# Attention's transposes split by head into pairs, and the early weight pieces spread over more units

## The chip, the cores and the metric

The kernel runs on one core of one Trainium2 chip. Its time is the device time of one execution in microseconds (us): before the change 389.75 us, the median of three runs (389.58 to 389.85). The core has a matrix engine (TensorE, PE in the profile; its weight loads are shown apart as PEld), VectorE (DVE), ScalarE (ACT), GpSimd (POOL), and SyncE (SP), which here issues nearly all DMA transfers. TensorE writes to PSUM, which has eight banks of 512 fp32 columns; the other data stands in SBUF, both with 128 partitions.

## The reference

Three layers follow each other, all in fp32.

```
y[t]  = r[t] @ (state + (u*k[t]) v[t]^T)          # 4 batches, 8 heads, 768 steps, head size 48
state = w * state + k[t] v[t]^T
x = y as 3072 tokens x 384
logits = x @ phi                                   # 32 slots, 8 experts of 4
d = softmax over tokens, c = softmax over slots
slot_out[e] = relu((d.T @ x)[e] @ w1[e]) @ w2[e]   # w1: 384 x 1024, w2: 1024 x 384
x = c @ slot_out
out = (relu(x @ w_in) ** 2) @ w_out                # 384 -> 2048 -> 384
```

## The kernel before

**Stages.** Up to about 28 us the kernel starts up; until about 127 us it computes the attention and, woven in, the softmax over the tokens; until about 160 us the experts; then the last layer, whose products take TensorE to the end.

**Attention in units.** A unit is one batch and a pair of heads: 16 units, four per batch. A unit's 768 steps are cut into NC = 6 chunks of 128. The recurrence is written as products: inside a chunk, A = K R^T (with decays multiplied in) is masked and multiplied with V; between chunks a state of 48 x 48 per head is carried by a scan. The data of a unit comes in one load of 1344 KB (`load_unit`, line 87): r and v with the steps on the partitions, and r and k turned, with head 0 in rows 0 to 47 and head 1 in rows 64 to 111.

**Even and odd chunks.** The chunks of a unit go through two PSUM banks, YE (even chunks) and YO (odd chunks), called `YB[0]` and `YB[1]`. `inter` (line 316) and `intra` (line 325) write the attention's result there, turned: head size on the partitions, steps on the columns. ScalarE copies each bank to `xT` (line 328). In the odd bank the two heads have changed places. The name kvp stands for one more bank, in which `KV` (line 298) builds the states in columns 0 to 287, and ps_tr for one that is free for short uses.

**Transposes.** `turns(x, k)`, lines 235 to 257, does two jobs with one set of banks. For the unit x (the one just finished) it turns `xT` back, so that the steps stand on the partitions, in `xn`, which the softmax stage reads. For the unit k (two ahead) it turns the decayed k into `kn`, which `pr2` on GpSimd and `KV` read one unit later. A full call has six transposes for each job, each of one chunk with both heads at once: 112 rows, of which 96 are used. They go to YE, YO and ps_tr; five copies of ScalarE (lines 252, 255, 257) take them out.

**The order of the work.** The order on each engine is written out by hand in one loop over the units n. TensorE does in this order: A(n, odd); `turns(n-1, n+2)`; in units 5, 9 and 13 four transposes more, `both` (line 373); A(n+1, even); `L(n-1)`, the logits (line 337); in units 6, 10 and 14 `soft3`; `inter(n)`; `KV(n+1)`; `intra(n)`, even and odd. A writes the two banks of ps_A (line 286), head 0 to the one and head 1 to the other; there is one ps_A. `cp` on VectorE (line 290, a COPY_PREDICATED) takes A out of it. VectorE does: `weigh(n+1)`, `cp(n, odd)`, `decay(n+3)`, `cp(n+1, even)`, `decay(n+2)`, `scan(n+1)`. In units 4, 8 and 12 ScalarE has the exponent of the softmax and one copy more (lines 348 and 350) between its copies of YE and YO. In the text below A(n, 1) stands for the odd chunks of unit n and A(n, 0) for the even ones.

**Loads.** At the end of unit n, SP issues the load of unit n+5 (five slots), and after it some pieces of 512 KB of the first eight expert weights (line 197): 24 pieces, of which three go at the start and 21 after units 0 to 10. From unit 11 on there are no more units to load; then come the other expert weights, 1536 KB each (line 194), into the slots that the units leave, and the first part of w_in.

The lines that set the places of these are, in the loop:

```
if n > 0 or nx2:
    turns(n - 1 if n > 0 else None, n + 2 if nx2 else None)
...
if nxt:
    A(n + 1, 0)
    cp(n + 1, 0)
```

Of the kernel before, what the change touches and what calls it, by code (L numbers as in the profile page):

```python
# [17 lines left out]
def rwkv_softmoe_ffn(ctx: ExitStack, tc: tile.TileContext, un, k0, wt, u, phi, w1, w2, w_in, w_out, out):  # L18
    nc = tc.nc
    NU, NPC, _, PW = un.shape  # L20
    H, D = u.shape
    NP = H // 2
    B = NU // NP
    DM, NTOK = out.shape
    S = NTOK // B
    NC = S // 128
    HC = NC // 2
# [7 lines left out]
    NB = 5  # L35
# [13 lines left out]
    def ps(tag, banks=1):  # L49
        cnt[0] += 1  # L50
        return psum.tile([128, 512 * banks], F32, name=f"ps_{tag}{cnt[0]}", tag=tag, bufs=BANKS.get(tag, 1))
# [8 lines left out]
    def take(i, dt=F32):  # L60
        if i in early:
            return early.pop(i)
        cnt[0] += 1
        slots[i] = const.tile([128, 3072], dt, name=f"slot{i}_{cnt[0]}", tag=f"slot{i}", bufs=1)
        return slots[i]
# [9 lines left out]
    def t_view(n):  # L75
        return units[n % NB][:112, ON:ON + OT].rearrange("p (m c t) -> p m c t", m=2, c=NC)
# [17 lines left out]
    def part_of(sh, rows, at, shape):  # L94
        n = 1
        for x in shape:
            n *= x
        dims = "abcd"[:len(shape)]
        return sh[:rows, at:at + n].rearrange(f"p ({' '.join(dims)}) -> p {' '.join(dims)}", **dict(zip(dims, shape)))
# [5 lines left out]
    xn = [part_of(sh0, 128, 0, [NC, DM + 1]), att.tile([128, NC, DM + 1], F32, name="xn1")]  # L105
# [14 lines left out]
    ident = const.tile([128, 128], F32, name="ident")  # L120
# [15 lines left out]
    st = {}  # L136
# [48 lines left out]
    def load_weight(i, cs=None):  # L185
        kind, e = W[i]
        if W[i] not in wt_of:
            t = take(home[i])
            wt_of[W[i]] = t.rearrange("p (c f) -> p c f", c=3) if kind == "w1" else t.rearrange("p (c d) -> p c d", c=8)
            st["raw", i] = t.rearrange("p (c f) -> p c f", c=3)  # L190
        t = st["raw", i]
        src = w1[e].rearrange("(c p) f -> c p f", p=128) if kind == "w1" else w2[e]
        if cs is None:
            nc.sync.dma_start(t, src.rearrange("c p f -> p c f"))
        else:
            for c in cs:
                nc.sync.dma_start(t[:, c], src[c])

    kvp = ps("kv")
    YB = [ps("YE"), ps("YO")]  # L200
# [10 lines left out]
    for i in range(6):  # L211
        n = 1 << i
# [19 lines left out]
    def heads(p):  # L232
        return p.rearrange("p c (h x) -> p c h x", h=2)[:, :, :, :D]

    def turns(x, k):
        banks = [YB[0], YB[1], ps("tr")]
        banks = [p.rearrange("p (c e) -> p c e", c=4) for p in banks]
        tail = [[NC - 2], [NC - 1], list(range(NC - 2))]
        if k is not None:
            kn = st[k, "kn"] = kns[(k + 1) % 2]  # L240
        for par, p in enumerate(banks):
            if x is not None and par < 2:
                for i in range(HC):
                    nc.tensor.transpose(p[:, i, :112], st[x, "xT"][:, par, i], ident[:112, :112])  # L244
            if k is not None:
                for j, c in enumerate(tail[par]):
                    nc.tensor.transpose(p[:, HC * (par < 2) + j, :112], t_view(k)[:, 1, c], ident[:112, :112])
        for par, p in enumerate(banks):
            if x is not None and par < 2:
                b, hp = divmod(x, NP)  # L250
                dst = xn[b % 2][:, par::2, 2 * D * hp:2 * D * (hp + 1)].rearrange("p c (h d) -> p c h d", h=2)
                nc.scalar.copy(dst[:, :, ::-1] if par else dst, heads(p[:, :HC]))
            if k is not None:
                if par < 2:
                    nc.scalar.copy(kn[:, NC - 2 + par], heads(p[:, HC:])[:, 0])
                else:
                    nc.scalar.copy(kn[:, :NC - 2], heads(p))  # L257

    def pr1(n):
        rv = r_view(n)  # L260
        nc.gpsimd.tensor_tensor(rv, rv, UT[:, n % NP].unsqueeze(1).to_broadcast([128, NC, 2, D]), ALU.mult)  # L261
# [5 lines left out]
    def weigh(n):  # L267
        dg = wk([128, 2, NC], "dg", 2)
        nc.vector.reduce_sum(dg, r_view(n).rearrange("p c h d -> p h c d"), axis=AX.X)
        st[n, "dg"] = dg  # L270

    def diag(n, par):
        at = wk([128, 2, HC, 128], "AT", 3, pool=att)
        st[n, "AT", par] = at
        dg = st[n, "dg"][:, :, par::2]
        nc.gpsimd.affine_select(out=at, in_=dg.unsqueeze(3).to_broadcast([128, 2, HC, 128]),  # L276
                                pattern=[[0, 2], [0, HC], [1, 128]], compare_op=ALU.is_equal, fill=0.0,
                                base=0, channel_multiplier=-1)

    def A(n, par):  # L280
        tv = t_view(n)
        p = ps("A", 2).rearrange("p (h x) -> p h x", h=2)[:, :, :HC * 128].rearrange("p h (c t) -> p h c t", c=HC)
        for i in range(HC):
            for h in range(2):
                rows = slice(64 * h, 64 * h + D)
                nc.tensor.matmul(p[:, h, i], tv[rows, 1, 2 * i + par], tv[rows, 0, 2 * i + par], start=True, stop=True)  # L286
        st[n, "A", par] = p

    def cp(n, par):
        nc.vector.copy_predicated(st[n, "AT", par], mask.unsqueeze(1).unsqueeze(1).to_broadcast([128, 2, HC, 128]),  # L290
                                  st.pop((n, "A", par)))
# [95 lines left out]
    def c_exp(b):  # L387
        nc.scalar.activation(cnat[:, b], cnat[:, b], AF.Exp)
# [87 lines left out]
    loads = [[] for n in range(NU)]  # L476
    pieces = [(i, c) for i in range(NEARLY) for c in range(3)]
    for _ in range(3):
        i, c = pieces.pop(0)
        load_weight(i, (c,))  # L480
    NL = NU - NB
    for j, pc in enumerate(pieces):
        loads[j * NL // len(pieces)].append(pc)
    for n in range(NU):
        nxt = n + 1 < NU
        nx2 = n + 2 < NU
        nx3 = n + 3 < NU
        prev = n // NP - 1
        hp = n % NP
        if n == 2:  # L490
            sel = const.tile([128, 4, NS], F32, name="sel")
            nc.vector.reduce_sum(sel, ident.rearrange("p (q s) -> p s q", q=4).unsqueeze(1).to_broadcast([128, 4, NS, 4]), axis=AX.X)
            rm = const.tile([128, E], F32, name="rm")
            nc.vector.reduce_sum(rm, ident.rearrange("p (q e j) -> p e q j", q=4, e=E), axis=AX.XY)
            ones = const.tile([1, 4], F32, name="ones")
            nc.gpsimd.memset(ones, 1.0)
        A(n, 1)
        if prev >= 0 and hp == 2:
            c_exp(prev)
        if nx2:  # L500
            pr1(n + 2)
        if nxt:
            weigh(n + 1)
            diag(n + 1, 0)
        cp(n, 1)
        if prev >= 0 and hp == 2:
            c_sum(prev)
        if n > 0 or nx2:
            turns(n - 1 if n > 0 else None, n + 2 if nx2 else None)
        if prev >= 0 and hp == 1:  # L510
            both(prev)
            soft1d(prev)
        if nx2:
            pr2(n + 2)
        if nx3:
            decay(n + 3, 1)
# [3 lines that stand above are left out]
        if n > 0:  # L520
            L(n - 1)
        if prev >= 0 and hp == 2:
            soft3(prev)
        if prev >= 0 and hp == 0:
            soft1a(prev)
            soft1c(prev)
        if prev >= 0 and hp == 1:
            c_max(prev)
        if nxt:
            diag(n + 1, 1)  # L530
        inter(n)
        if nxt:
            KV(n + 1)
        if nx2:
            decay(n + 2, 0)
        if nxt:
            scan(n + 1)
        intra(n, 0)
        if prev >= 0 and hp == 0:
            soft1b(prev)  # L540
        intra(n, 1)
        if prev >= 0 and hp == 1:
            c_sub(prev)
        if prev >= 0 and hp == 2:
            c_div(prev)
            soft4(prev)
        if n + NB < NU:
            load_unit(n + NB)
            for i, c in loads[n]:
                load_weight(i, (c,))  # L550
        else:
            if n == NU - 2:
                load_win(0, take(NSLOT, I32))
            if n == NU - 1:
                load_weight(NSLOT)
            load_weight(NEARLY + n - NL)
# [7 lines left out]
    p = ps("kv")  # L564
# [6 lines left out]
    p = ps("kv")  # L571
# [9 lines left out]
    for c, bank in enumerate((YB[0], YB[1], ps("A", 2))):  # L581
        p = bank[:96, :cols[c].stop - cols[c].start]
# [167 lines left out]
    p = ps("tr")  # L750
# [102 lines left out]
    for i, (sg, f, half) in enumerate(order):  # L853
# [42 lines left out]
        for j, k in mms:  # L896
            o = acc[half][j]
            nc.tensor.matmul(o, (hi, lo, hi)[k][:, 128 * j:128 * (j + 1)], (gh, gh, gl)[k],  # L898
                             start=(f == 0 and k == 0), stop=(f == NF - 1 and k == 2))
            if f == NF - 1 and k == 2:  # L900
                tok = 512 * (2 * sg + half)
                os = oss[(3 * (2 * sg + half) + j) % 5]
                if i < NI - 2:
                    for e in range(2):
                        c = slice(256 * e, 256 * e + 256)
# [60 lines left out]
```

## Time and profile before

| | |
|---|---|
| median of the runs | 389.75 us (389.58 to 389.85) |
| profiled execution | 390.21 us, span of its instructions 388.5 us |
| busy share of the span | PE 97%, PEld 78%, DVE 69%, ACT 52%, POOL 28% |
| mean granted TensorE clock | 0.978 of full speed |
| DMA | 66.25 MB, 171 GB/s over the span |

The profile page divides the span of one execution; a timeline gives each run of like instructions with its start, its length and, in brackets, the idle time of its engine before it and what ended that. A group such as `ps_A<-slot` names the tile written and the tile read, with the buffer numbers left out. Products on PE are pipelined: the next one starts before the one ahead has ended, so a row's length is from the first start to the last end, and one product's own length is longer than the distance to the next.

### The profile page before, as it was taken

The numbers are of one execution on the slowest core, as the hardware profiler recorded it, in microseconds if no ns is written. First come the engines' busy times: TensorE is split into PE (matmuls) and PEld (weight loads), VectorE is DVE, ScalarE is ACT, GpSimd is POOL, SyncE is SP. The second block draws the span as 40 slices with busy tenths as digits, with TensorE's granted clock in tenths as the row PEclk, the third lists the DMA queues.
The fourth block names the chain that finished last, engine by engine and source line by source line (L and its number), as shares of the span: only waits on it lengthen the run. The fifth ranks groups of instructions, "written<-read, shape, count | busy, mean of one in ns | idle before, by whom it ended". The sixth has DMA issues, their size and how long they took to land.

```text
span 388.5 us, 8227 instructions
## 1 busy us (share of the span) xinstructions
PE 376.7 (97%) x3339; PEld 303.2 (78%) x3339; DVE 268.0 (69%) x437; ACT 203.0 (52%) x422; POOL 108.6 (28%) x115
## 2 busy tenths in 40 slices
PE   6889999999999999999999999999999999999996
PEld 4778888887887655688787888888888888888884
DVE  5669788788874368589987677665665676566663
ACT  2213343444252333399787866555555565555553
POOL 4566675867761312043422240000000000000000
PEclk9559999999999999999999999999999999999999
DMA  6979999999969999813242203000000040000004
GB/s 237 390 295 356 387 375 379 329 391 311 334 200 364 412 372 397 299 55 98 84 104 90 64 0 139 24 0 0 2 1 0 2 163 0 2 0 0 2 1 163
DMA packets 23174, 66.25 MB, mean 171 GB/s; under 512 B 3296, under 2 KB 4832, under 8 KB 23136
## 3 DMA queue, kind: packets, MB, share of 16 engines
q1 hardware_dynamic: 22848, 65.38, 45.7%
q8 instruction: 26, 0.43, 0.4%
q10 hardware_dynamic: 288, 0.34, 0.3%
q14 instruction: 12, 0.10, 0.1%
HBM read 60.21 MB, written 4.72 MB: 167 GB/s over the span
## 4 chain that ended last, share of the span: by engine, by line
PE 92%; DMA 4%; DVE 2%; issue 1%; ACT 0%; ACTq 0%; DVEq 0%
PE ps_A L898 25%; PE ps_Y L898 9%; PE ps_kv L898 8%; PE ps_lg L898 8%; PE ps_A L286 7%; PE ps_tr L803 6%; PE ps_YO L316 3%; PE ps_YE L325 3%; PE ps_YO L325 3%; PE ps_A L618 3%; PE ps_Y L639 3%; DMA slot<-in_un_dram 3%; PE ps_kv L298 2%; PE ps_lg L337 2%; PE ps_YE L244 2%; DMA slot<-in_u_dram 2%
## 5 line engine op out<-in xcount | busy, mean ns | idle before, releaser
L827 DVE TENSOR_TENSOR slot<-slot,slot 128x512 fp32r<-128x512 f32 (+1 forms) x97 | 69.5, 717 | 53.3 <-PE ps_A L898 18.6
L898 PE MATMUL ps_A<-slot,slot 128*128 128x512 f32 x432 | 105.8, 389 | 0.0
L898 PEld LDWEIGHTS ps_A<-slot,slot 128*128 128x128 f32 x432 | 81.0, 188 | 17.2 <-ACT slot L824 0.3
L824 ACT CAST slot<-slot 128x512 fp32r<-128x512 f32 (+1 forms) x97 | 59.7, 616 | 49.5 <-DVE slot L821 49.2
L814 ACT ACTIVATE slot<-ps_tr 128x512 f32<-128x512 f32 (+1 forms) x97 | 57.5, 593 | 22.9 <-PE ps_tr L803 22.0
L821 DVE TENSOR_TENSOR slot<-slot 128x512 f32<-128x512 f32 (+1 forms) x71 | 48.4, 683 | 11.5 <-ACT slot L814 11.3
L898 PE MATMUL ps_Y<-slot,slot 128*128 128x512 f32 x144 | 55.4, 391 | 0.0
L898 PE MATMUL ps_kv<-slot,slot 128*128 128x512 f32 x144 | 55.1, 389 | 0.0
L898 PE MATMUL ps_lg<-slot,slot 128*128 128x512 f32 x144 | 55.0, 389 | 0.0
L290 DVE COPY_PREDICATED AT<-mask,ps_A 128x768 f32<-128x768 int32 x32 | 33.8, 1055 | 16.9 <-PE ps_A L286 9.8
L803 PE MATMUL ps_tr<-slot,slot 128*128 128x512 f32 x96 | 37.4, 391 | 0.4 <-DVE slot L767 0.4
L276 POOL TENSOR_SCALAR_AFFINE_SELECT AT<-dg 128x768 f32<-128x768 f32 x32 | 28.3, 887 | 31.8 <-PE ps_YE L325 30.3
L286 PE MATMUL ps_A<-slot 48*128 48x128 f32 x384 | 32.2, 303 | 4.7 <-DVE slot L230 3.1
L683 POOL TENSOR_TENSOR slot<-wf,slot 128x384 fp32r<-128x384 f32 x16 | 22.3, 1395 | 51.6 <-ACT slot L678 49.6
L286 PEld LDWEIGHTS ps_A<-slot 48*128 48x128 f32 x384 | 25.7, 200 | 10.9 <-DVE slot L230 3.7
L230 DVE TENSOR_TENSOR slot<-slot,ps_tab 112x768 f32<-112x768 f32 (+1 forms) x34 | 30.2, 894 | 5.1 <-DMA slot<-in_un_dram 5.1
L898 PEld LDWEIGHTS ps_Y<-slot,slot 128*128 128x128 f32 x144 | 27.0, 188 | 5.9 <-issue 0.4
L898 PEld LDWEIGHTS ps_kv<-slot,slot 128*128 128x128 f32 x144 | 27.0, 188 | 5.7
L898 PEld LDWEIGHTS ps_lg<-slot,slot 128*128 128x128 f32 x144 | 27.0, 188 | 5.5
L328 ACT COPY xT<-ps_YE 112x384 f32<-112x384 f32 x16 | 7.7, 479 | 43.3 <-PE ps_YE L325 43.3
L265 POOL TENSOR_TENSOR slot<-slot,slot 128x576 f32<-128x576 f32 x16 | 22.7, 1416 | 7.7 <-ACT slot L257 7.6
L261 POOL TENSOR_TENSOR slot<-slot,slot 128x576 f32<-128x576 f32 x15 | 21.3, 1421 | 0.3 <-ACT slot L458 0.3
(192 smaller groups left out, 503.6 us busy)
## 6 DMA issues: line engine op xcount, KB each, us to landing
slot<-in_un_dram SPq DMA_DIRECT2D x15, 1344.0 KB, 7.8
slot<-in_w_dram SPq DMA_DIRECT2D x24, 512.0 KB, 8.8
slot<-in_w_dram SPq DMA_DIRECT2D x8, 1536.0 KB, 9.4
slot<-in_w_in_dram SPq DMA_DIRECT2D x4, 1536.0 KB, 8.4
wo<-in_w_out_dram SPq DMA_DIRECT2D x16, 384.0 KB, 3.2
out_dram<-slot SPq DMA_DIRECT2D x18, 256.0 KB, 2.1
slot<-in_un_dram SPq DMA_DIRECT2D x3, 448.0 KB, 6.7
slot<-slot SPq DMA_DIRECT2D x48, 16.0 KB, 1.9
```

The lines of the kernel that those rows point to most:

```text
L230: nc.vector.tensor_tensor(x, x, t.unsqueeze(1).to_broadcast(list(x.shape)), ALU.mult)
L265: nc.gpsimd.tensor_tensor(rv, rv, st[n, "kn"] if by is None else by, ALU.mult)
L276: nc.gpsimd.affine_select(out=at, in_=dg.unsqueeze(3).to_broadcast([128, 2, HC, 128]), pattern=[[0, 2], [0, HC], [1, 128]], compare_op=ALU ...
L286: nc.tensor.matmul(p[:, h, i], tv[rows, 1, 2 * i + par], tv[rows, 0, 2 * i + par], start=True, stop=True)
L290: nc.vector.copy_predicated(st[n, "AT", par], mask.unsqueeze(1).unsqueeze(1).to_broadcast([128, 2, HC, 128]), st.pop((n, "A", par)))
L325: nc.tensor.matmul(p[o:o + D, i], vv[:, 2 * i + par, h], at[:, h, i], start=False, stop=True, skip_group_check=True)
L803: nc.tensor.matmul(p, gst[:, 128 * f:128 * (f + 1)], cTall[:, 512 * g:512 * (g + 1)], start=True, stop=True)
L814: nc.scalar.activation(fs[i, "hr"][:, c], fs[i, "p"][:, c], AF.Relu)
L821: nc.vector.tensor_mul(gg, hr, hr)
L824: nc.scalar.copy(part(i, "gh")[:, c], fs[i, "gg"][:, c])
L827: nc.vector.tensor_tensor(part(i, "gl")[:, c], fs[i, "gg"][:, c], fs[i, "gh"].bitcast(F32)[:, c], ALU.subtract)
L898: nc.tensor.matmul(o, (hi, lo, hi)[k][:, 128 * j:128 * (j + 1)], (gh, gh, gl)[k], start=(f == 0 and k == 0), stop=(f == NF - 1 and k == 2))
```

## The change

`turns` no longer turns both heads of a chunk at once. Each transpose has the 48 rows of one head (rows 0 to 47, or 64 to 111) and 48 moving columns. The transposes of the two heads are issued in pairs, and the two of a pair write different banks: for x, head rows 0 to 47 go to YE and head rows 64 to 111 to YO; for k, the one half goes to ps_tr, of the other two chunks to YO and four to columns 288 to 479 of the kvp bank. The chunks of x are taken even, odd, even, odd. Five copies of ScalarE remain, with other cuts; `turned` gives the place in `xn` for each half, over even and odd chunks. The second part of the change lets the 21 weight pieces run over units 0 to 13; in units 11 to 13 they are issued ahead of the 1536 KB loads.

```diff
+    def turned(x, a):
+        b, hp = divmod(x, NP)
+        v = xn[b % 2][:, ::2, D * (2 * hp + a):D * (2 * hp + a + 1)].unsqueeze(2)
+        pairs = [list(e) for e in v.ap]
+        return bass.AP(v.tensor, v.offset, [pairs[0], pairs[1], [DM + 1 - 2 * D * a + D, 2], pairs[3]])
+
     def turns(x, k):
-        banks = [YB[0], YB[1], ps("tr")]
-        banks = [p.rearrange("p (c e) -> p c e", c=4) for p in banks]
-        tail = [[NC - 2], [NC - 1], list(range(NC - 2))]
+        rows = [slice(64 * a, 64 * a + D) for a in range(2)]
+        todo = [[], []]
+        if x is not None:
+            px = [YB[a][:, :NC * D].rearrange("p (i q d) -> p i q d", q=2, d=D) for a in range(2)]
+            for a in range(2):
+                todo[a] += [(px[a][:, i, q], st[x, "xT"][rows[a], q, i]) for i in range(HC) for q in range(2)]
         if k is not None:
             kn = st[k, "kn"] = kns[(k + 1) % 2]
-        for par, p in enumerate(banks):
...
+            to = [ps("tr")[:, :NC * D], YB[1][:, NC * D:NC * D + 2 * D], kvp[:, NC * D:NC * D + 4 * D]]
+            to = [p.rearrange("p (c d) -> p c d", d=D) for p in to]
+            parts_k = [(0, slice(0, NC), to[0]), (1, slice(0, 2), to[1]), (1, slice(2, NC), to[2])]
+            for a, cs, p in parts_k:
+                todo[a] += [(p[:, i], t_view(k)[rows[a], 1, c]) for i, c in enumerate(range(NC)[cs])]
+        for pair in zip(*todo):
+            for a, (o, i) in enumerate(pair):
+                nc.tensor.transpose(o, i, ident[rows[a], rows[a]])
+        for a in range(2):
+            if x is not None:
+                nc.scalar.copy(turned(x, a), px[a])
+        if k is not None:
+            for a, cs, p in parts_k[1:] + parts_k[:1]:
+                nc.scalar.copy(kn[:, cs, a], p)
...
-        loads[j * NL // len(pieces)].append(pc)
+        loads[j * (NL + 3) // len(pieces)].append(pc)
...
         if n + NB < NU:
             load_unit(n + NB)
-            for i, c in loads[n]:
-                load_weight(i, (c,))
-        else:
+        for i, c in loads[n]:
+            load_weight(i, (c,))
+        if n + NB >= NU:
```

## Rows read from the trace of the kernel before

**Rows 1.** The page's chain that ended last, by engine

```profile
PE 92%; DMA 4%; DVE 2%; issue 1%; ACT 0%; ACTq 0%; DVEq 0%
```

**Rows 2.** Timeline of unit 12: start us, length us, engine, line, tiles, form, count

```profile
100.93 0.94 PE L286 MATMUL ps_A<-slot 48*128 48x128 f32 x12
...
101.80 0.51 PE L244 MATMUL ps_YE<-ident,xT 112*128 112x112 f32 x3
101.97 1.07 DVE L290 COPY_PREDICATED AT<-mask,ps_A 128x768 f32<-128x768 int32 x1 [0.66 <-POOL AT L276]
...
102.62 0.55 PE L247 MATMUL ps_tr<-ident,slot 112*128 112x112 f32 x4
...
103.10 0.94 PE L286 MATMUL ps_A<-slot 48*128 48x128 f32 x12
```

**Rows 3.** Timeline of unit 3, the copy and the next A

```profile
41.72 1.06 DVE L290 COPY_PREDICATED AT<-mask,ps_A 128x768 f32<-128x768 int32 x1 [0.84 <-POOL AT L276]
...
42.85 0.38 PE L286 MATMUL ps_A<-slot 48*128 48x128 f32 x2
```

**Rows 4.** Timeline of unit 14, which has six transposes

```profile
113.92 0.94 PE L286 MATMUL ps_A<-slot 48*128 48x128 f32 x12
...
114.98 1.05 DVE L290 COPY_PREDICATED AT<-mask,ps_A 128x768 f32<-128x768 int32 x1 [0.70 <-PE ps_A L286]
...
115.14 0.45 PE L244 MATMUL ps_YO<-ident,xT 112*128 112x112 f32 x3
...
116.08 0.49 PE L286 MATMUL ps_A<-slot 48*128 48x128 f32 x3 [0.49 <-DVE AT L290]
```

**Rows 5.** Timeline of unit 13, with `both` (L373) between transposes and A

```profile
107.72 0.49 ACT L328 COPY xT<-ps_YO 112x384 f32<-112x384 f32 x1
...
108.32 1.06 DVE L290 COPY_PREDICATED AT<-mask,ps_A 128x768 f32<-128x768 int32 x1 [0.44 <-PE ps_A L286]
...
109.34 0.49 PE L373 MATMUL ps_lg<-ident,el 96*128 96x96 f32 x4
...
109.76 0.38 PE L286 MATMUL ps_A<-slot 48*128 48x128 f32 x2
```

**Rows 6.** Single products, ns min/median/max; and timeline of KV and end sum

```profile
L244 PE MATMUL ps_YE<-ident,xT x48: 259/259/318, 28.7 to 127.2; 112*128 112x112 f32 x48
L286 PE MATMUL ps_A<-slot x384: 272/272/579, 10.7 to 122.2; 48*128 48x128 f32 x192
105.36 0.66 PE L298 MATMUL ps_kv<-slot,slot 128*48 128x48 f32 x20
L591 PE MATMUL ps_kv<-m,P x12: 276/276/297, 130.4 to 131.7; 96*128 96x32 f32 x12
130.43 1.52 PE L591 MATMUL ps_kv<-m,P 96*128 96x32 f32 x12
```

**Rows 7.** Chain of waits at the end of the start: start us, us, what

```profile
20.23 0.95 DVE AT L290
...
21.23 1.65 PE ps_A L286 x12
```

**Rows 8.** DMA by stretch (last columns share, GB/s); late weights; VectorE's waits; chain

```profile
34.00:60.00 26.00, 25.85 (x456) 22.03 (x452) 22.27 (x29) 10.29 (x32) 18.13 (x18) 1.00 1.00 379
104.00:120.00 16.00, 15.51 (x283) 12.46 (x283) 10.90 (x17) 6.28 (x19) 8.09 (x8) 1.00 0.78 275
L194 SPq DMA_DIRECT2D slot<-in_w_dram x8: 367/368/379, 101.0 to 136.8; - x8
DMA to landing us min/median/max: 6.2/9.4/14.8
152.30 5.30 PE ps_Y L639 x64
DVE slot L658 <- PE ps_kv L655: 2.7, 1, 2.7
DVE wf L157 <- DMA wo<-in_w_out_dram: 0.8, 1, 0.8
```

More of the change, by code (lines that the diff above doesn't have):

```diff
@@ L239, in turns @@
+    def turns(x, k):
+        rows = [slice(64 * a, 64 * a + D) for a in range(2)]
[4 more added lines that the diff above has]
+                todo[a] += [(px[a][:, i, q], st[x, "xT"][rows[a], q, i]) for i in range(HC) for q in range(2)]
         if k is not None:
             kn = st[k, "kn"] = kns[(k + 1) % 2]
-        for par, p in enumerate(banks):
[L242 to L255, printed above, removed]
-                else:
-                    nc.scalar.copy(kn[:, :NC - 2], heads(p))
+            to = [ps("tr")[:, :NC * D], YB[1][:, NC * D:NC * D + 2 * D], kvp[:, NC * D:NC * D + 4 * D]]
@@ L548, in rwkv_softmoe_ffn @@
             load_unit(n + NB)
-            for i, c in loads[n]:
-                load_weight(i, (c,))
-        else:
+        for i, c in loads[n]:
+            load_weight(i, (c,))
+        if n + NB >= NU:
             if n == NU - 2:
```

## The prediction

> **What bounds the kernel now.** I read the page's chain first: PE is 92% of the chain that ended last [rows 1]. Taken alone that says that any TensorE time saved is time won. So I went on to the stretch that the change touches, the 16 attention units, and read the timeline of one whole unit, 12, instead of the shares [rows 2]. Its PE order is A(12,1), twelve transposes (`turns`), A(13,0), L, and on. A(12,1) starts at 100.93 and A(13,0) at 103.10: 2.17 us. The reader is to see two things in that gap. PE fills it: the twelve transposes run from 101.80 to 103.17. And VectorE fills it too: the masked copy `cp` (L290) reads ps_A from 101.97 to 103.04, and A(13,0) overwrites ps_A, of which there is only one buffer. A(13,0) starts 0.06 after that copy ends. The same stands in units 1 to 4, 6 to 8 and 10 to 12, ten units, where the distance is 0.05 to 0.07 each time; unit 3 is shown [rows 3].
>
> Which of the two holds A back? Unit 14 answers: it has six transposes instead of twelve (there is no unit 16 to prepare), its last one starts at 115.14 + 0.45 - 0.26 = 115.33 (0.26 is a transpose's own length), and yet A(15,0) waits 0.49 us on PE for the copy and starts 0.05 after it ended [rows 4]. From the start of A to the start of the next A it takes 116.08 - 113.92 = 2.16 us, although half of the transposes are gone. That is the floor: A, copy, A. So in ten units PE's transposes and the copy end together, and cutting only the transposes buys nearly nothing.
>
> Three units differ, 5, 9 and 13. There four more transposes (L373, `both`) stand between `turns` and A, and A starts at 109.76 where the copy ended at 109.38 [rows 5]. There PE alone is late, by 0.38 - 0.05 = 0.33 us; units 5 and 9 read the same to 0.02.
>
> **The change part by part.** *Transposes.* A full `turns` has 12 transposes of 112 rows and 112 moving columns; the change makes 24 of 48 rows and 48 moving columns, in 12 pairs. Before, one follows the other at (0.55 - 0.26)/3 = 0.096 us [rows 2, 6], 1.06 us from the first to the last start, plus 0.06 for the first load (the longest takes 318 ns, the usual one 259) [rows 6].
> After, no row has a pair of transposes. The nearest: A runs two 48-row products beside each other, in two banks, 12 in 0.94 us; with 0.27 for the last and 0.10 for the first load (its first pair takes 0.38, the usual 0.27) that is 0.114 us for a pair with 128 moving columns [rows 2, 3, 6]. KV, with 48 moving columns and loads of 48, takes 0.66 us for ten pairs with the whole length of the last [rows 6], some 0.05 a pair without it: the low end. The end sum, with 32 moving columns and single loads of 128 columns, takes (1.52 - 0.276)/11 = 0.113 us each [rows 6]: the high end, if the two loads of a pair go together. I take 0.063, since a pair is bound by its load of 128 columns, a transpose's load shows as 0.06, and A shows two row halves loading together. So 12 pairs need 0.06 + 11 x 0.063 = 0.75 us where 1.11 were needed.
> In the ten units PE is done some 0.45 us before the copy and waits. What is late next is the copy, which needs A's last product (0.1 us after A's end) and 1.06 us of VectorE. Gain: what A now starts above 0.054 after the copy, 0 to 0.02 in each, 0.08 us for all ten.
> In units 5, 9 and 13 the new order has a wait of its own: the first pair already writes bank YO, so it cannot start before ScalarE has copied YO, and in these units that copy ends late, at 107.72 + 0.49 = 108.21 [rows 5]; the old order begins with YE, copied earlier. Behind that pair on PE stand all others, `both` and A. With 0.05 from ScalarE to PE, as from VectorE to PE in rows 4, the first pair starts at 108.26, the last at 108.26 + 0.06 + 11 x 0.063 = 109.01. Before, the last of the twelve started 0.10 ahead of `both`, at 109.24, so from the last transpose to A it took 0.52. Now `both` (96 rows) follows 48-row work, and a change of that kind costs: from the last transpose's start to A's it is 0.19, against 0.096 inside the run [rows 2]. I add 0.1: A at 109.01 + 0.62 = 109.63, 0.13 earlier than 109.76. Bounds: 0 and 0.33 (the copy). Three units: 0.4 us, 0 to 1.0.
>
> The Trainium skill, TensorEngine Tiling (Array Packing), section Key Properties, says that a change of tiling mode drains the engine. It speaks for the change between A and `turns`, which would then share a mode, and against it at `both`, a new change; without that drain the three units would give 0.7 instead of 0.4. The 0.19 against 0.096 agrees with it.
>
> *ScalarE.* Five copies of 1152 elements a partition in all, as before (288, 96, 288, 96 and 384 against 288, 288, 96, 192 and 288). Their ends move by a tenth at most; behind the last one waits only POOL's product, whose own result is first read in the unit after. Zero.
> *Start and end.* The start is bound elsewhere: A(1,0) at 21.23 follows the copy on VectorE [rows 7], which stands behind VectorE's work on the unit loads. In unit 15 the next work that needs `turns` is inter, behind ScalarE's copies of xn, and both copies then wait for all six pairs instead of three transposes of one bank; six pairs need about what three old ones took. Zero, or six times what a pair is slower than 0.063, which is +0.3 at 0.113.
> *Weight pieces.* 21 pieces of 512 KB after units 0 to 13, not 0 to 10: by unit 10 17 are issued instead of 21. On SP the last four now stand ahead of the 1.5 MB weight loads that follow units 11 to 13; those wait for a unit to free its slot (the first goes at 101.0 [rows 8]), and SP has nothing else in that time, so four more issues delay none of them. What they can delay is on the DMA queues. DMA was 100% busy from 34 to 60 us and 78% from 104 to 120 [rows 8], so the pieces go where there is room. The list of waits from 28 to 124 us has none on a unit load, so relief buys nothing. If the later loads slip: the last w2, issued at 136.8 and landed at most 14.8 later, at 151.6, is used in the last quarter of the downs that start at 152.30 and take 5.30, so some 4.6 us remain; the first w_out, for which VectorE waits 0.8, has 2.7 us of VectorE's idle time behind it [rows 8]. Four pieces are 2.1 MB, at 379 GB/s 5.5 us, of which the idle 22% of 16 us take 3.5; a slip of 2 us is left, under both margins. Zero, at worst +0.5, should it come on top of another delay.
>
> Sum: -0.08 - 0.4 = -0.5 us on the profiled 390.21 us (span 388.5 and 1.7 around it); the median of the runs, 389.75, is 0.46 below that execution, and I take the difference to it: **389.3 us**.
>
> **The rivals.**
> *Faster: the three units give all they can.* No drain at `both`, pairs near 0.05: 3 x 0.33 + 0.08 = 1.1 us, 388.65. For it: KV's 0.05. Against it: the late YO copy, and loads of 128 columns.
> *Much faster: the copy doesn't hold A.* Then 0.45 to 0.55 us in each of 14 units, 7 us, 382.5. Against it: unit 14.
> *Slower: the pairs are slow.* A starts late from the point where the last pair starts after 102.99 (103.10 less 0.11): with a first start at 101.71 (0.114 after A's last, 101.60) from (102.99 - 101.77)/11 = 0.111 us a pair. If a transpose's load costs what the end sum's does (0.113, first load 0.10), ten units lose 0.07, three 0.45 and unit 15 0.3: +2.3, 392.0. If the two halves don't overlap, 24 x 0.063: ten units lose 0.2, three 0.6, unit 15 0.4: +4.2, 394.0. Against both: A's pairs, and the first load's 0.06.
> The Trainium skill, TensorE: Matmul & The Clock Gate, section LDWEIGHTS, gives a load's time by its columns whatever its rows: for 128 columns an estimate of 107 ns; by that rule the time would be the 392.0 of the first of these two. Its first transpose in a run, only 59 ns longer, disagrees.
> *The weight pieces bind.* VectorE's w_out wait grows past its 2.7 us: some +0.5, 390.25.
>
> **How the numbers follow.** Forecast 0.60; the weight pieces, also no measurable change, 0.04; the three units in full or more 0.21, of which the 7 us are 0.02; slow pairs 0.15. About 0.2%, 0.8 us, is what a measurement of this kernel can tell from no change. Faster 0.21, same 0.64, slower 0.15. The range reaches to the fast rival below and halfway to the first slow one above: 388.4 to 391.4.
>
> **What would show it.** After: A(n+1,0) still starts 0.05 to 0.07 after the end of L290 in the plain units, now with PE idle 0.3 to 0.5 us before it, released by DVE AT L290; the A to A distance there stays 2.16. Pairs of transposes start 0.06 apart. In units 5, 9 and 13 the first pair waits for ACT L328. DMA's share between 34 and 60 us falls. Wrong would be: A earlier than the copy's end, pairs above 0.11, or a new wait for a load after 120 us.

## The result and the profile after

The changed kernel takes 392.30 us, median of 20 runs (389.91 to 396.33), against 389.77 of the kernel before (20 runs beside them, 389.28 to 390.46). It is slower: the ratio is 1.0056, interval 1.0033 to 1.0079. The forecast was 389.3 within 388.4 to 391.4; the time lies outside, on the side to which 0.15 was given. The runs fall in three groups: six at 389.9 to 390.5, seven at 392.1 to 393.0, seven at 395.6 to 396.3. Their mean granted clocks go with the groups: 0.977 to 0.978, 0.972 to 0.974, 0.964 to 0.965. The ratio leaves out runs more than 1.5% above the fastest of their kernel, so five of the last group are not in it. The profiled execution took 392.22 us, span 390.4, mean granted clock 0.972 (before 390.21, 388.5 and 0.978).

In the kernel after, A is at line 292, `cp` at 296, the transposes at 257, the copies of x at 260, those of k at 263, L at 343, `both` at 379 and its copy out of ps_lg at 381, the end sums (the last batch's sums over the tokens and what joins them to the rest, ahead of the experts) at 591, 597 and 602, the experts' first products at 624.

A plain unit went as foreseen. This is the timeline of unit 12 after (start us, length us, engine, line, operation, tiles, form, count, and idle time before it with its releaser); it answers to [rows 2].

```profile
101.06 0.94 PE L292 MATMUL ps_A<-slot 48*128 48x128 f32 x12
101.83 0.20 PE L257 MATMUL ps_YE<-ident,xT 48*128 48x48 f32 x1
...
101.94 0.22 PE L257 MATMUL ps_YE<-ident,xT 48*128 48x48 f32 x1
...
102.10 1.05 DVE L296 COPY_PREDICATED AT<-mask,ps_A 128x768 f32<-128x768 int32 x1 [0.77 <-POOL AT L282]
...
102.49 0.22 PE L257 MATMUL ps_kv<-ident,slot 48*128 48x48 f32 x1
...
103.21 0.94 PE L292 MATMUL ps_A<-slot 48*128 48x128 f32 x12 [0.49 <-DVE AT L296]
```

The pairs start 0.06 us apart, the last one at 102.49; PE then waits 0.49 us for the masked copy, and A follows 0.06 after its end, 2.15 us after the A before (2.17 in [rows 2]). The waits of PE between 28 and 124 us (total us, times, longest) name it once before and eleven times after, first before, then after:

```profile
PE ps_A L286 <- DVE AT L290: 0.5, 1, 0.5
```

```profile
PE ps_A L292 <- DVE AT L296: 6.5, 11, 0.9
PE ps_lg L343 <- ACT nat L381: 0.6, 3, 0.2
```

The last of these lines was not foreseen. It stands in units 5, 9 and 13. The timeline of unit 13 after answers to [rows 5]:

```profile
107.37 0.94 PE L292 MATMUL ps_A<-slot 48*128 48x128 f32 x12
107.83 0.49 ACT L334 COPY xT<-ps_YO 112x384 f32<-112x384 f32 x1
...
108.37 0.14 PEld L257 LDWEIGHTS ps_YO<-ident,xT 48*128 48x128 f32 x1 [0.20 <-ACT xT L334]
...
109.24 0.55 PE L379 MATMUL ps_lg<-ident,el 96*128 96x96 f32 x4
...
109.72 0.94 PE L292 MATMUL ps_A<-slot 48*128 48x128 f32 x12
...
110.29 0.52 ACT L381 COPY nat<-ps_lg 128x384 f32<-128x384 f32 x1
...
110.86 0.64 PE L343 MATMUL ps_lg<-xT,phs 112*32 112x128 f32 x12 [0.20 <-ACT nat L381]
```

A(14,0) comes 109.72 - 107.37 = 2.35 us after A(13,1) instead of 2.50, as forecast. But L starts 1.14 us after A(14,0). Before, ScalarE's copy out of ps_lg started at 109.99, and L followed A(14,0) by 0.87:

```profile
109.76 0.94 PE L286 MATMUL ps_A<-slot 48*128 48x128 f32 x12
109.99 0.54 ACT L375 COPY nat<-ps_lg 128x384 f32<-128x384 f32 x1
...
110.63 0.64 PE L337 MATMUL ps_lg<-xT,phs 112*32 112x128 f32 x12
```

The largest part is behind the attention. These are stretches of 1 us (window, length, PE busy us and count, granted clock, DMA share, GB/s), first before, then after:

```profile
127.00:128.00 1.00, 0.92 (x10) 1.00 1.02 414
128.00:129.00 1.00, 0.72 (x7) 1.00 1.00 397
129.00:130.00 1.00, 1.00 (x29) 1.00 1.03 422
130.00:131.00 1.00, 1.00 (x20) 1.00 1.00 410
```

```profile
127.00:128.00 1.00, 0.88 (x18) 1.00 1.03 406
128.00:129.00 1.00, 0.61 (x3) 1.00 1.02 393
129.00:130.00 1.00, 0.93 (x14) 0.74 0.99 369
130.00:131.00 1.00, 1.00 (x21) 0.50 1.02 410
131.00:132.00 1.00, 1.00 (x16) 0.50 1.03 422
132.00:133.00 1.00, 1.00 (x9) 0.55 1.03 422
133.00:134.00 1.00, 1.00 (x12) 1.00 0.99 406
```

After, the granted clock goes from 1.00 (2.4 GHz) to 0.50 (1.2 GHz) in the middle of 129 to 130 and is back by 133; before, it stays at 1.00. The end sums run in that time. Groups of PE between 126.5 and 136 (busy us, mean ns of one), before and after:

```profile
L591 PE MATMUL ps_kv<-m,P 96*128 96x32 f32 x12 | 1.5, 278 | 0.0
L585 PE MATMUL ps_A<-xn,en 128*32 128x129 f32 x12 | 0.6, 273 | 0.0
```

```profile
L597 PE MATMUL ps_kv<-m,P 96*128 96x32 f32 x12 | 1.9, 319 | 0.0
L591 PE MATMUL ps_A<-xn,en 128*32 128x129 f32 x12 | 1.1, 422 | 0.0
```

Distances between the first products of one A and the next, from the timelines, give the account (us; steps left out differ by 0.02 at most, and most by under 0.005):

| Step | before | after | difference |
|---|---|---|---|
| eight odd A to even A in units 3, 4, 6, 7, 8, 10, 12, 14 | 17.34 | 17.22 | -0.11 |
| A(2,1) to A(3,0) | 2.39 | 2.54 | +0.15 |
| units 5, 9, 13: A(n,1) to A(n+1,0) | 7.50 | 7.05 | -0.45 |
| units 5, 9, 13: A(n+1,0) to A(n+1,1) | 12.49 | 13.30 | +0.81 |
| A(11,1) to A(12,0) | 2.17 | 2.46 | +0.29 |
| A(15,1) to the experts' first product | 11.09 | 12.85 | +1.76 |

Together +2.45 us; the medians differ by 2.5. The start, up to A(2,0), is not in it (29.97 us in the profile before, 29.49 after): where the clock first rises varies from execution to execution (27.8 us and 27.1). The weight pieces went as foreseen: DMA's busy share from 34 to 60 us fell from 1.00 to 0.93, and behind 120 us the list of waits names no load any more.

### The profile page after: what moved, and what is told of

It is laid out like the page before. It is cut to its first block, busy times and chain, and to the rows that moved or that the text cites. A ratio compares the mean times of both kernels' runs of the same rounds, so it can differ in the third digit from the quotient of the medians.

```text
span 390.4 us, 8647 instructions
## 1 busy us (share of the span) xinstructions
PE 370.2 (95%) x3531; PEld 298.4 (76%) x3531; DVE 268.9 (69%) x437; ACT 204.5 (52%) x422; POOL 108.7 (28%) x115
## 4 chain that ended last, share of the span: by engine, by line
PE 84%; DVE 5%; DMA 4%; issue 2%; ACT 2%; POOL 1%; ACTq 0%; DVEq 0%
PE ps_A L904 25%; PE ps_Y L904 8%; PE ps_kv L904 8%; PE ps_lg L904 8%; PE ps_tr L809 6%; PE ps_A L292 5%; PE ps_YO L322 3%; DVE AT L296 3%; PE ps_A L624 3%; PE ps_YE L331 3%; PE ps_Y L645 3%; DMA slot<-in_un_dram 2%; PE ps_kv L304 2%; PE ps_lg L343 2%; DMA slot<-in_u_dram 2%
```

## The experiments

Each was timed in five rounds beside the kernel before. In all, that kernel ran 86 times beside these kernels, from 388.93 to 391.24; none was near 392, and where the clock is on record (66 of them) it is 0.978 or more. The theory to begin with: the pairs thin TensorE's work in the last call of `turns` (unit 15, after the loop), the clock falls, and the rest is waits that the split makes in the units. The rivals: the weight pieces; the thinner work of all units; a stall in the tail.

**The pieces alone.**

```
 if n + NB < NU:
     load_unit(n + NB)
-    for i, c in loads[n]: ...       # and pieces over NL units
+for i, c in loads[n]: ...           # over NL + 3; turns as before
```

> Only the weight pieces are spread over units 0 to 13; the transposes are those of the kernel before. Theory (the loss comes from the transposes: less TensorE work between 126 and 130 us, after which the granted clock falls to half in the end sums): no loss, 389.8 +- 0.4 us, the granted clock stays at full after 28 us. Rival (the later weight pieces hold something up): 391.5 or more, with a wait for a DMA after 120 us.

390.06 us (12 runs), ratio 1.0009 (0.9997 to 1.0021); clock 0.978, and every step in the table above as before, to 0.015 us. The pieces do nothing that these runs can tell.

**The transposes alone** (the change without `NL + 3`).

> Only the transposes are changed; the weight pieces go as in the kernel before. Theory: the whole loss, executions between 390 and 396 us as with both changes, median about 392, and in those over 391.5 a stretch of half clock near 130 us. Rival (the pieces): 389.8.

392.43 us (9 runs, 390.07 to 397.01), ratio 1.0048 (1.0013 to 1.0083), with the same steps in the units as the full change. The loss is the transposes'. The profiled execution is the longest of them: its clock is at 0.50 from 132 on, and still in most of 136 to 142:

```profile
131.00:132.00 1.00, 1.00 (x25) 0.81 1.01 414
...
136.00:142.00 6.00, 5.75 (x55) 0.51 0.55 178
```

So the fall can last longer than in the profile of the change. This profile has the clock 0.960, the group near 396 has 0.964 to 0.965, against 0.972 in the profile of the change. So that group's clocks point to the longer fall; the profile with only the last call in pairs, below, has one of that length at 0.964.

**The last call whole.**

```
-    turns(NU - 1, None)
+    turns_whole(NU - 1, None)       # the turns of the kernel before
```

> The changed kernel, but the last call of turns, the one behind the loop (unit 15, six transposes), does whole 112-row transposes as before. Theory (it is the TensorE work just ahead of the fall that decides): the clock stays, 390.1 +- 0.3 us in nearly all executions. Rival (the work lost in the loop, or the pairs themselves, lets the clock fall): 392 and scattered as with the change.

390.46 us (12 runs, 389.90 to 391.28), ratio 1.0018 (1.0007 to 1.0029). The profile has no fall, and, since part of the runs of the change have none either, more to the point: all twelve runs have the clock 0.977 or more, and the scatter over three groups is gone. From A(15,1) to the experts it takes 11.18 us. So of the 1.76 us of the tail, 1.67 are the clock's; the other 0.09 stay. The median stays 0.61 us above the kernel before (389.85 beside it); the units' rows of the table give +0.69, and the tail the 0.09.

**Filler.** The change, with three products that nobody reads, after the last call.

```
+    filler = ps("A", 2)
+    for _ in range(3):
+        nc.tensor.matmul(filler[:, :128], ident, ident, start=True, stop=True)
```

> The changed kernel with three extra products of 128 columns behind the last call of turns; their result is not used. [...] Theory: 390.1 +- 0.3 us as with whole transposes in the last call, although more work is done. Rival (what whole transposes of the last call give back is something else, such as the copies' order): stays at 392.

391.22 us (10 runs, 390.61 to 391.85), ratio 1.0037 (1.0024 to 1.0049); no fall in the profile, the clock 0.977 or more in all ten runs, no run over 392. More work for TensorE keeps the clock, though nothing else of the change is undone. It costs time itself: 0.94 us of products stand ahead of the transpose for the maximum on PE, and A(15,1) to the experts takes 11.58, 0.40 more than with the last call whole. The expected 390.1 was missed by 1.1; the rest of that is not explained. The products also put in more work than the pairs had taken out, so the run does not show how much is needed.

**Only the last call in pairs**, all else as before.

```
-    turns(NU - 1, None)
+    turns_split(NU - 1, None)       # the turns of the change
```

> The kernel before, with the pairs in the last call alone (the six of unit 15 after the loop); all other calls whole, weight pieces as before. Theory that this one call decides whether the granted clock falls in the tail: the clock goes to half level somewhere in 128 to 134 us of the profile or in part of the runs, and the times scatter over 389.9 to 396 with a median near 392. Rival, that the fall needs the whole attention's thinner TensorE load (pairs in all units): no fall, 389.85 as the kernel before, or 390.0 with the second xn copy 0.1 later.

394.39 us (6 runs: two at 390.9 and 391.0, four at 394.3 to 394.6), ratio 1.0087 (1.0055 to 1.012). Six pairs in place of six transposes bring the fall alone (the clock is 0.964 in the four long runs, 0.972 and 0.978 in the two short ones), and the rival that all units are needed falls. A(15,1) starts at 121.54 in the kernel before and at 121.14 here, so the same work lies 0.40 us earlier. These are the stretches from 6 to 7 us behind A(15,1), first before, then here, and behind them the fall:

```profile
127.54:128.54 1.00, 0.86 (x6) 1.00 1.03 414
```

```profile
127.14:128.14 1.00, 0.64 (x5) 1.00 1.04 410
```

```profile
129.00:130.00 1.00, 1.00 (x27) 0.65 1.02 414
130.00:131.00 1.00, 1.00 (x13) 0.50 1.00 406
```

PE is busy 0.64 us where the kernel before has 0.86; between 129 and 130 the clock goes down. Here it stays at 0.50 until some 139.5 (0.70 over 136 to 142), and from A(15,1) to the end of the span it takes 4.8 us more than before. The rest of the scatter, that some executions have no fall, a short or a long one, is not explained.

**Late copies.** With the last call whole, and in units 5, 9 and 13:

```
-        for a, cs, p in ...: nc.scalar.copy(kn[:, cs, a], p)      # three copies of k
+        ...                                                       # the first one
         both(prev)
+            for o, i in late: nc.scalar.copy(o, i)                # the other two
```

> The changed kernel with the last call whole (390.46 us alone in an earlier run), and in units 5, 9 and 13 two of ScalarE's three copies of k (those out of ps_tr and ps_kv) issued after the copy that frees ps_lg. Theory: in these units the logits product of the unit before waits for ScalarE's copy out of ps_lg, which the split calls put later, so A(6,1), A(10,1) and A(14,1) come 0.27 us late each: with the copies moved, the steps A(6,0), A(10,0), A(14,0) to the next A fall from 4.43 to about 4.17 us and the total by about 0.8, to 389.65. Rival: those steps are long for another reason (GpSimd's product with the turned k, which now waits longer for the moved copies): steps stay at 4.43 or grow, total 390.4 to 390.8.

In all three units the step behind the call fell from 4.43 to 4.16 us, as the theory has it. The copy out of ps_lg now starts at 109.84, and L follows A(14,0) by 0.87 again:

```profile
109.73 0.94 PE L322 MATMUL ps_A<-slot 48*128 48x128 f32 x12
109.84 0.48 ACT L411 COPY nat<-ps_lg 128x384 f32<-128x384 f32 x1
...
110.60 0.64 PE L373 MATMUL ps_lg<-xT,phs 112*32 112x128 f32 x12
```

The median, 390.27 (6 runs), ratio 1.0005 (0.9989 to 1.002), is higher than the 389.65 expected; six runs with this scatter don't hold 0.8 us, so the steps are the evidence.

**Unit 11 whole**, and then **unit 10 whole**, each on top of the late copies.

```
+            if n == 11:      # in the second kernel: n == 10
+                turns_whole(n - 1, n + 2)
+            else: ...        # pairs, as in the late copies
```

> The kernel of e6_late_copies with the transposes of unit 11 whole again (no copy out of ps_kv there). Theory: the 0.29 us in A(11,1) to A(12,0) come from VectorE's scan, which behind a split call waits for ScalarE's copy out of ps_kv as well and starts 0.07 us later, so that GpSimd's selection starts ahead of VectorE's weight update, which then takes 1.24 us instead of 0.59: with that call whole the update takes 0.59 again, the step falls from 2.46 to 2.17 and the total lies 0.3 below e6_late_copies. Rival, that the order has flipped because everything before lies elsewhere in time: step stays at 2.46, total the same as e6_late_copies.

> e6_late_copies (390.27 us) with the transposes of unit 10 whole, those of unit 11 pairs again: unit 10's call, not unit 11's, fills ps_kv last before the scan of unit 12 that runs in unit 11. Theory: the scan waits for ScalarE's copy out of ps_kv because of that call; with it whole the scan comes 4.27 instead of 4.34 us after A(11,0), VectorE's weight update stands ahead of GpSimd's selection again and takes 0.59 instead of 1.24 us, the step A(11,1) to A(12,0) falls from 2.46 to 2.17 and the total by 0.3, to about 390.0. Rival: the order flips from what the units before have shifted: scan at 4.34, update 1.24, step 2.46, total 390.3.

The first missed: the step A(11,1) to A(12,0) stayed at 2.46 (389.62 us, ratio 0.9991, 0.9976 to 1.0006). I had picked the wrong call. The scan that is late is the one for unit 11, which runs in unit 10 (the expectations name unit 12), and what fills ps_kv last before it is the call in unit 10. With that one whole the step is 2.16 (389.67 us, 12 runs, ratio 0.9998, 0.9988 to 1.0007). The timelines, after and with unit 10 whole:

```profile
93.31 0.76 DVE L308 TENSOR_TENSOR_SCAN slot<-ps_kv,slot 112x288 f32<-112x288 f32 x1 [0.58 <-PE ps_kv L304]
93.94 0.87 POOL L282 TENSOR_SCALAR_AFFINE_SELECT AT<-dg 128x768 f32<-128x768 f32 x1 [2.69 <-PE ps_YE L331]
93.98 1.24 DVE L440 SCALAR_TENSOR_TENSOR P<-P,fa,pb 96x385 f32<-96x385 f32 x1
```

```profile
93.05 0.76 DVE L338 TENSOR_TENSOR_SCAN slot<-ps_kv,slot 112x288 f32<-112x288 f32 x1 [0.54 <-PE ps_kv L334]
93.72 0.59 DVE L470 SCALAR_TENSOR_TENSOR P<-P,fa,pb 96x385 f32<-96x385 f32 x1
93.75 1.30 POOL L312 TENSOR_SCALAR_AFFINE_SELECT AT<-dg 128x768 f32<-128x768 f32 x1 [2.70 <-PE ps_YE L361]
```

Counted from A(11,0), the scan starts at 4.335 us behind a split call and at 4.267 behind a whole one, while `KV` ends at 4.218 in both. GpSimd's selection starts at 4.96 in both. So 0.07 us decide which of the two is first: VectorE's update behind the selection takes 1.24 us, ahead of it 0.59, and then it is the selection that takes 1.30 instead of 0.87. So the split call of unit 10 delays the scan. The trace also shows by what. With the change VectorE has one instruction more at this scan's line, a wait for a semaphore, at 4.271, and the scan starts 0.064 after it; with the call whole there is none:

```profile
L308 DVEq EVENT_SEMAPHORE  x1: 21/21/21, 93.2 to 93.2; - x1
```

It waits for `KV`, and the scan itself then for ScalarE, whose copy out of ps_kv shares the bank. That copy had ended 4.0 us before the scan, so nothing is waited for there: the extra instruction is what the scan is late by. In the profile after, the eight scans with it start 0.116 to 0.117 us behind the end of `KV`; four without it start 0.047 to 0.048 behind it.

**Pairs where PE is late.** Pairs in units 5, 9 and 13 only, k's four pairs into ps_tr and ps_kv first, the late copies; whole transposes elsewhere.

```
-            todo[a] += [...]                                  # x's pairs, then k's
+            todo = [of_k[a][:4] + todo[a] + of_k[a][4:] for a in range(2)]
```

> Pairs only in units 5, 9 and 13, the first four of them k's (into ps_tr and ps_kv, which wait for nothing of ScalarE), the two late copies of k behind the copy that frees ps_lg; whole transposes everywhere else, weight pieces spread as in the change. Theory: each of the three steps A(n,1) to A(n+1,0) falls from 2.50 to between 2.16 (the floor by the masked copy) and 2.35, the steps after them stay at 4.17, unit 11 stays at 2.17 and the clock does not fall: 389.85 less 0.45 to 1.0, so 388.85 to 389.4, faster than the kernel before. Rival, that the transposes' gain is given back in every unit later whatever is done: 389.85.

> The kernel of e10_pairs_in_three_units again, for the interval: the steps say 1.0 us below the kernel before (three steps of 2.50 to 2.16), the earlier runs 0.3 (389.58 against 389.89, interval of the ratio 0.9976 to 1.0008), with the start up to the rise of the clock different in each execution. If the steps hold, the median is 388.9 to 389.4 and the ratio under 1; rival, no difference: 389.85.

First 389.58 us (6 runs), ratio 0.9992 (0.9976 to 1.0008), unclear; again, 389.06 (12 runs), ratio 0.9975 (0.9964 to 0.9985): faster by 0.25%. The timeline of unit 13, from the first of the two profiles, shows why:

```profile
107.61 0.49 ACT L362 COPY xT<-ps_YO 112x384 f32<-112x384 f32 x1
107.92 0.20 PE L258 MATMUL ps_tr<-ident,slot 48*128 48x48 f32 x1
...
108.16 0.25 PE L258 MATMUL ps_YO<-ident,xT 48*128 48x48 f32 x1
108.21 1.06 DVE L324 COPY_PREDICATED AT<-mask,ps_A 128x768 f32<-128x768 int32 x1 [0.44 <-PE ps_A L320]
...
109.32 0.94 PE L320 MATMUL ps_A<-slot 48*128 48x128 f32 x12
```

Four pairs of k fill the time until ScalarE has copied YO (108.10), and A starts 0.05 after the masked copy: in both profiles all three steps are at 2.16 to 2.18 us, the floor, from 2.50. One of the first six runs, 390.63 us, has the clock 0.972, the only one below 0.976 of the 62 runs of all kernels here with the last call whole; it has no profile, so where its clock was low is not known.

**Combined.** Pairs everywhere but in unit 10 and the last call, with k first and late copies in units 5, 9 and 13.

> Pairs everywhere but in unit 10 and the last call, late copies and k's four pairs first in units 5, 9 and 13. From the steps read so far: three steps of 2.50 fall to 2.16 (-1.0 us together), eight plain steps by 0.02 each (-0.15), A(2,1) to A(3,0) grows by 0.15, end of the attention +0.1: 389.85 less 0.9, about 389.0. Rival, that the freed time is taken by the scatter of the start or given back in later units: 389.85.

388.84 us (8 runs), ratio 0.9971 (0.9959 to 0.9984): it beats both kernels. It is not told apart from the one with pairs in three units only, so the pairs in the plain units need not be there.

## Why the prediction was wrong

**Right: the plain units.** The copy holds A, the floor of 2.16 us stands, and the freed time became a wait of PE. Eight steps gave 0.11 us.

**Right: the pairs.** 0.062 us apart against 0.063. The rival of slow pairs is out. By the Trainium skill, TensorE: Matmul & The Clock Gate, section LDWEIGHTS, the estimate was 107 ns for one load of 128 columns; here a load's own row is 0.14 us long, but loads overlap, and two of them with their products start every 62 ns, so the measurement decides.

**Right, but counted too short: units 5, 9 and 13.** "A at 109.01 + 0.62 = 109.63, 0.13 earlier than 109.76": measured 0.15 in each, 0.45 in all against 0.4, behind the forecast wait for ScalarE's copy of YO. The sum stopped at A. The next step on PE is L, which writes ps_lg, and the copy that frees ps_lg stands behind five copies on ScalarE. The step "ScalarE ... Their ends move by a tenth at most; behind the last one waits only POOL's product" failed: the copy out of ps_lg is queued there too, and it came 0.57 instead of 0.23 us after A(14,0). That cost 0.27 us in each unit, nearly twice what was won, and the late copies took it away. In the sum up to A, the 0.1 us added ahead of `both` came out (0.15 from the last transpose, 109.09, to `both`, against 0.06 inside the run), but by luck: the 0.19 it was read from holds A's wait for the masked copy, which ends 0.06 ahead of A in [rows 2].

**Missing: unit 11, +0.29.** No step had the bank that `KV` and the transposes now share. Only 0.07 us of it is delay, of the scan's extra wait instruction; the rest comes from the changed order of GpSimd and VectorE. The Trainium skill, Trainium Architecture — The Big Picture, section What this means for kernel authors, says that these two share a port under an exclusive lock; the durations of 1.24 and 1.30 us for whichever came second agree with it in kind; each is some 0.15 us shorter than a full wait behind the other would make it.

**Missing: A(2,1) to A(3,0), +0.15.** It was not tried by itself; it is absent where the calls of units 1 and 2 are whole (2.37 with pairs in three units only). The traces show half of it: the scan in unit 1 has the same extra instruction and ends 0.07 us later, and VectorE has no gap behind it. The other 0.08 arises between VectorE's sum in `weigh` and the masked copy and stays open.

**Wrong: "Start and end ... Zero".** This step weighed unit 15 by its waits and did not price the call after the loop at all, and it put the clock at nothing: it quotes no row on the granted clock behind 120 us. That call decides the result: whole, no profile has a fall, and alone in pairs there is one. In the change's profile the fall is worth 1.67 us; a fall of some 10 us is worth about 4.8 in the profile with only the last call in pairs, and the group near 396 lies 5.7 us above the one near 390. The waits that the step did weigh cost 0.09. What could be read beforehand is thin work just ahead of the end sums: PE busy 0.92 and 0.72 us of the two from 127 to 129 in the kernel before, between waits for VectorE and ScalarE. The last call in pairs takes 0.22 us out of this stretch; that this is enough for a fall no row of the kernel before could say. The Trainium skill, TensorE: Matmul & The Clock Gate, section HAM oscillation — how this bites in real kernels, ties a fall to gaps in which the engine idles; PE's longest gaps between 126 us and the fall are these (timeline after), 0.30 and 0.28 us, so by that section a fall was not to be expected here, and the measurement decides.

```profile
128.18 0.24 PE L571 MATMUL ps_kv<-ident,m 96*1 96x96 f32 x1 [0.30 <-DVE m L567]
...
129.07 0.30 PE L578 MATMUL ps_kv<-ones,m 1*96 1x2 f32 x2 [0.28 <-DVE m L574]
```

**Two numbers of the prediction do not follow from its own words.** Halfway from 389.3 to the first slow rival, 392.0, is 390.7 and not 391.4, and 389.75 less 7 is 382.75 and not 382.5. The result lies outside either range.

## What to carry to other kernels

Where TensorE's work is thin, a cheaper form of it can cost more than it saves: read the granted clock and the busy time in the stretch before each dense part, and leave slow but dense work there. When a step is to start earlier, follow its engine to the next instruction behind it, and look up who frees what that one writes. Put a faster form only where its engine is the one that is late; here three units of sixteen.

## What the runs showed that was not expected

Two transposes of 48 rows with 48 moving columns, in two row halves and two banks, start every 0.062 us. A second semaphore to wait for, even one long reached, brings a VectorE scan one instruction more and 0.07 us. Of a VectorE operation with two tensors read and a GpSimd selection that overlap, the later one pays: 0.59 to 1.24 us, or 0.87 to 1.30, decided by 0.07 us. And the clock's fall in the tail lasted some 3.4 us in one profile and some 10 us in two others, and by times and clocks part of the runs of the same kernel had none. In all three profiles the fall came 102.40 us after the clock had risen (27.08 to 129.48 us with the change, 29.23 to 131.63 with the transposes alone, 26.91 to 129.31 with only the last call in pairs), while A(15,1) stood 7.7, 8.3 and 8.2 us ahead of it; what that means for the runs without a fall is not shown.
